# Row factors of two chunks by a VectorE block transpose and DMA instead of matmuls, with the first values tile moved

## The chip, the cores and the metric

One core of one Trainium2 chip. The metric is the device time of one execution in microseconds. The kernel before takes 206.06 us (median of the first three runs, 206.0 to 206.29).

## The reference, cut to what matters

```python
def _B_ref(x, w1, w2, w3, w4):
    h = _gelu(_layernorm(x, axis=-1) @ w1)
    ...                                   # shifts over rows, w2, a second layer norm, w3, w4
x = A_x
xn = _layernorm(x, axis=-1)
s = _A_ref(xn, A_wqkv, A_wo)              # dilated sliding-window attention
g = _silu(_B_ref(xn, B_w1, B_w2, B_w3, B_w4))
return x + s * g
```

x is 2048 rows by 512. The layer norm is applied twice in a row ahead of w1: once for xn and once more inside `_B_ref`. The second one is a factor for each row alone, since the mean of xn is zero. The kernel works in four chunks of 512 rows and holds xn transposed (features over partitions), so a factor for each row is a factor for each *column* there: it has to be turned from one value per partition into one row, repeated over all 128 partitions.

## The kernel before: the parts concerned

```python
def ln_again(c):                     # the factors of chunk c, [128, 4], a column for each tile
    ...
    eng = nc.vector if c == 3 else nc.gpsimd
    ...                              # r2 = rstd*rstd*var + EPS, small operations
    r2b = small.tile([P, TPC], BF16, name="r2b", tag="r2b")
    nc.gpsimd.tensor_tensor(out=r2b, in0=r2, in1=nhalf, op=ALU.pow)      # "the power"
    r2s[c] = r2b

def stage_r(c):                      # turn and spread by four matmuls, then a ScalarE copy
    rp = psb("rrep_ps")
    r2 = r2s.pop(c)
    for j in range(TPC):
        nc.tensor.matmul(rp[:, j * P : (j + 1) * P],
                         lhsT=r2[:, j : j + 1].to_broadcast([P, P]), rhs=ident[:],
                         start=True, stop=True)
    nc.scalar.copy(out=xn2T[c][:, ND - 1, :], in_=rp)

def stage_m(c):                      # "the multiplication": input of w1
    ...                              # rrep = xn2T[c][:, ND - 1, :], the row; cs: columns of chunk c
    nc.vector.tensor_tensor(out=xn2T[c], in0=xnT[p][:, :, cs],
                            in1=rrep.unsqueeze(1).to_broadcast([P, ND, CH]), op=ALU.mult)

# ... program order of the prologue, cut
    turn_dma(2)()                    # xn of chunk 2 to DRAM and back by a DMA transpose
    ln_again(2)
    stage_w1(0, 1)
    mask_full(1)
    mask_fill(0, (0,))               # "the fill copies": two VectorE copies of 128x2048
    for a in range(2):
        qk_pair(1, a)[0]()
    stage_r(1)
    stage_m(1)
    ln_stats(3, 0, 2)
    ...
    stage_w1(1, 0)
    stage_w1(1, 1)
    stage_r(2)
    stage_t(3, 0)                    # transposes of chunk 3 on TensorE
    ln_norm(3, slice(1, 2))
    stage_m(2)
    ln_again(3)
    qk_pair(2, 0)[0]()
    ...
    stage_w1(2, 0, lambda: stage_r(3))
    ...
    va = values(0, 0)                # then the first scores
```

In the timelines the instructions of VectorE and of TensorE start in this order.

The softmax here doesn't subtract the row's maximum and nothing guards it: scores larger than these inputs give would overflow.

## Time and profile before

| | before |
|---|---|
| span in the profile | 204.1 us |
| TensorE busy | 96% |
| VectorE, ScalarE, GpSimd busy | 66%, 64%, 37% |
| first scores start | 46.52 us |

```profile
2.81 0.69 DVE L304 BATCH_NORM_STATS2 l0s<-arena 128x6 f32<-128x512 bf16 x1 [0.90 <-DMA arena<-in_A_x_dram]
46.52 0.42 PE L567 MATMUL s_ps<-arena 32*128 32x128 bf16 x16
```

### The profile page before, as it was taken

The numbers are of one execution on the slowest core, as the hardware profiler recorded it, in microseconds if no ns is written. First come the engines' busy times: TensorE is split into PE (matmuls) and PEld (weight loads), VectorE is DVE, ScalarE is ACT, GpSimd is POOL, SyncE is SP. The second block draws the span as 40 slices with busy tenths as digits, with TensorE's granted clock in tenths as the row PEclk, the third lists the DMA queues.
The fourth block names the chain that finished last, engine by engine and source line by source line (L and its number), as shares of the span: only waits on it lengthen the run. The fifth ranks groups of instructions, "written<-read, shape, count | busy, mean of one in ns | idle before, by whom it ended". The sixth has DMA issues, their size and how long they took to land.

```text
span 204.1 us, 4800 instructions
## 1 busy us (share of the span) xinstructions
PE 195.2 (96%) x1900; PEld 94.9 (47%) x1928; DVE 135.0 (66%) x256; ACT 131.5 (64%) x157; POOL 74.5 (37%) x149
## 2 busy tenths in 40 slices
PE   7899999999999999999999999999999999999990
PEld 2585445444444444444444444444555444444440
DVE  5788897626298988856930101288577968888693
ACT  2366768657988888896556657898788877212130
POOL 5889842100023095964691000003830590700000
PEclk9999999999999999999999999999999999999997
DMA  5992264577900089495798948794220241553312
GB/s 146 356 348 80 87 139 86 85 109 112 275 34 5 14 199 140 75 254 107 181 196 184 295 148 136 109 278 156 36 51 5 56 89 26 116 165 118 117 51 77
DMA packets 33197, 26.74 MB, mean 131 GB/s; under 512 B 14600, under 2 KB 31088, under 8 KB 33176
## 3 DMA queue, kind: packets, MB, share of 16 engines
q1 hardware_dynamic: 30984, 23.22, 44.8%
q0 software_dynamic: 2048, 3.09, 8.9%
q8 instruction: 15, 0.25, 0.5%
q10 hardware_dynamic: 144, 0.13, 0.2%
q14 instruction: 6, 0.05, 0.1%
HBM read 12.40 MB, written 4.98 MB: 85 GB/s over the span
## 4 chain that ended last, share of the span: by engine, by line
PE 71%; DVE 11%; DMA 9%; issue 3%; POOL 3%; ACT 2%; SPq 0%; DVEq 0%; POOLq 0%
PE w_ps L501 19%; PE w_ps L521 10%; PE v_ps L547 8%; PE s_ps L567 7%; PE w_ps L457 6%; PE qk_ps L401 5%; PE w_ps L434 5%; PE o_ps L590 4%; PE qk_ps L419 4%; DMA den_d<-orw 3%; PE wo_ps L683 3%; DMA arena<-rden_d 2%; DVE arena L537 2%; DMA rden_d<-rb 1%; DVE arena L691 1%
## 5 line engine op out<-in xcount | busy, mean ns | idle before, releaser
L572 ACT ACTIVATE arena<-s_ps 128x960 bf16<-128x960 f32 (+1 forms) x68 | 62.7, 975 | 13.7 <-PE s_ps L567 13.7
L521 PE MATMUL w_ps<-arena 128*128 128x512 bf16 (+1 forms) x156 | 38.5, 380 | 0.6 <-issue 0.2
L506 ACT ACTIVATE arena<-w_ps 128x1024 bf16<-128x1024 f32 x20 | 20.5, 1024 | 14.5 <-PE w_ps L501 13.1
L632 POOL DMA_DIRECT2D arena<-orw x48 | 25.0, 528 | 5.8 <-DVE orw L602 5.8
L501 PEld LDWEIGHTS <-arena 128*128 128x128 bf16 (+1 forms) x176 | 17.5, 100 | 20.5 <-issue 0.4
L521 PEld LDWEIGHTS <-arena 128*128 128x128 bf16 (+1 forms) x176 | 16.5, 98 | 19.5
L693 POOL TENSOR_TENSOR arena<-arena 128x512 bf16<-128x512 bf16 x6 | 7.7, 1302 | 44.4 <-DVE arena L691 44.4
L536 ACT ACTIVATE sig<-arena 128x512 bf16<-128x512 bf16 x16 | 10.1, 631 | 21.0 <-DVE arena L527 20.9
L551 DVE CAST v_aug<-v_ps 128x512 bf16<-128x512 f32 x17 | 11.7, 690 | 15.4 <-PE v_ps L547 15.3
L602 DVE CAST orw<-o_ps 128x960 bf16<-128x960 f32 (+1 forms) x17 | 19.7, 1156 | 3.1 <-PE o_ps L590 3.0
L401 PE MATMUL qk_ps<-arena 128*128 128x512 bf16 (+1 forms) x109 | 20.4, 332 | 0.5 <-ACT arena L321 0.3
L501 PE MATMUL w_ps<-arena 128*128 128x512 bf16 (+1 forms) x86 | 19.4, 379 | 0.2
L501 PE MATMUL w_ps<-arena,arena 128*128 128x512 bf16 (+1 forms) x86 | 19.1, 379 | 0.1
L547 PE MATMUL v_ps<-wv_sb,arena 128*128 128x512 bf16 x67 | 17.5, 380 | 0.1
L567 PEld LDWEIGHTS <-arena 32*128 32x128 bf16 x544 | 10.2, 92 | 14.8 <-issue 14.7
L567 PE MATMUL s_ps<-arena 32*128 32x120 bf16 (+1 forms) x544 | 16.1, 213 | 0.1
L527 DVE TENSOR_TENSOR arena<-w_ps,arena 128x512 bf16<-128x512 f32 x16 | 11.0, 686 | 7.9 <-PE w_ps L521 7.9
L273 POOL TENSOR_SCALAR l3r<-l3m 128x1 f32<-128x1 f32 (+1 forms) x10 | 2.4, 238 | 37.6 <-DVE l3m L282 37.6
L457 PE MATMUL w_ps<-arena 128*128 128x512 bf16 x63 | 15.2, 380 | 0.1
L660 DVE TENSOR_TENSOR arena<-arena,orw 128x1440 bf16<-128x1440 bf16 (+1 forms) x2 | 1.6, 783 | 19.8 <-DMA orw<-rden_d 19.8
L434 PE MATMUL w_ps<-arena 128*128 128x512 bf16 x63 | 14.6, 379 | 0.0
L401 PEld LDWEIGHTS <-arena 128*128 128x128 bf16 x112 | 10.6, 98 | 7.9 <-DMA arena<-in_A_wqkv_dram 0.8
(99 smaller groups left out, 273.4 us busy)
## 6 DMA issues: line engine op xcount, KB each, us to landing
x1n_dram<-arena SPq DMA_DIRECT2D x5, 512.0 KB, 3.0
arena<-in_A_x_dram SPq DMA_DIRECT2D x4, 512.0 KB, 6.1
arena<-in_A_x_dram SPq DMA_DIRECT2D x6, 256.0 KB, 6.6
out_dram<-arena SPq DMA_DIRECT2D x6, 256.0 KB, 3.6
arena<-in_B_w_dram SPq DMA_DIRECT2D x1, 1376.0 KB
arena<-in_B_w_dram SPq DMA_DIRECT2D x1, 1280.0 KB
arena<-arena SPq DMA_DIRECT2D x16, 72.0 KB, 2.6
arena<-arena SPq DMA_DIRECT2D x16, 68.0 KB, 4.0
```

What stands on the lines that cost most here:

```text
L401: nc.tensor.matmul(pt[:, b, hh * w : (hh + 1) * w], lhsT=wqk_sb[:, dt, nt * P : (nt + 1) * P], rhs=xnT[p][:, dt, k * CH + hh * w : k * CH ...
L434: nc.tensor.matmul(pt[:, b, :], lhsT=w1_sb[:, dt, g * P : (g + 1) * P], rhs=xn2T[c][:, dt, :], start=(dt == 0), stop=(dt == ND - 1),)
L457: nc.tensor.matmul(pt, lhsT=w2_src(p, g, m0), rhs=w2_sb[:, g, :], start=(g == 0), stop=(g == ND - 1))
L501: nc.tensor.matmul(pt[:fs, ft % 2, :], lhsT=w3_sb[:, dt, ft * P : ft * P + fs], rhs=x1nT[c][:, dt, :], start=(dt == 0), stop=(dt == ND - 1),)
L506: nc.scalar.activation(h3(c, 2 * a, 2), pt, AF.Gelu_apprx_tanh)
L521: nc.tensor.matmul(pt, lhsT=h3(c, ft, 1)[:fs, 0, jj * P : (jj + 1) * P], rhs=w4_sb[:fs, ft, :], start=(ft == 0), stop=(ft == NF - 1),)
L547: nc.tensor.matmul(vp[:nk, :], lhsT=xnT[p][:, dt, k0 : k0 + nk], rhs=wv_sb[:, dt, :], start=(dt == 0), stop=(dt == ND - 1),)
L551: nc.vector.tensor_copy(out=va[:nk, :, 0:DH], in_=vp[:nk, :].rearrange("p (h d) -> p h d", d=DH))
L567: nc.tensor.matmul(st[:nk, b, i * nq : (i + 1) * nq], lhsT=kT[e][r : r + 32, dt, k0 : k0 + nk], rhs=qT[e][r : r + 32, dt, q0 : q0 + nq], s ...
L572: nc.scalar.activation(prv[:nk, 2 * h : 2 * h + 2], st[:nk, :, 0 : 4 * nq], AF.Exp, scale=SCALE)
L602: nc.vector.tensor_copy(out=orw[p, r][:, :, :, q0 - ra : q0 - ra + nq], in_=op[:, :, 0 : 4 * nq].rearrange("p j (s q) -> p j s q", q=nq),)
L632: nc.gpsimd.dma_start(out=oT[p][DH * hh : DH * (hh + 1), :, ra : ra + rw], in_=orw[p, r][32 * cg : 32 * cg + DH, jj],)
```

## The change

It takes the row spread of chunks 1 and 2 off TensorE. The four columns of factors are written into columns 0, 32, 64 and 96 of a zeroed 128x128 tile; one VectorE transpose by 32x32 blocks makes four rows of them; one DMA writes these to DRAM, a second reads them back over all partitions. The first values tile is moved from before the first scores to the place where chunk 2's spread was, and chunk 3's factors ahead of chunk 2's multiplication. The diff, cut:

```diff
+    def row_turn(c):
+        turned = small.tile([P, TPC, 32], BF16, name=f"r2t{c}", tag="r2t", bufs=1)
+        nc.vector.transpose(out=turned..., in_=r2w...)
+        row = dram.tile([TPC, P], BF16, name=f"r2_d{c}")
+        nc.sync.dma_start(out=row.rearrange("t (g i) -> g t i", g=4), in_=turned[0:P:32])
+        r2s[c] = row
+    def row_fill(c):
+        nc.sync.dma_start(out=xn2T[c][:, ND - 1, :], in_=r2s.pop(c)...to_broadcast([P, CH]))
...
     stage_t(1, 1)
+    row_turn(1)
+    row_fill(1)
...
-    turn_dma(2)()
+    turn = turn_dma(2)
     ln_again(2)
     stage_w1(0, 1)
     mask_full(1)
     mask_fill(0, (0,))
+    row_turn(2)
+    turn()
+    row_fill(2)
     for a in range(2):
         qk_pair(1, a)[0]()
-    stage_r(1)
     stage_m(1)
...
-    stage_r(2)
+    va, v_out = values(0, 0, True)
     stage_t(3, 0)
     ln_norm(3, slice(1, 2))
+    v_out()
+    ln_again(3)
     stage_m(2)
-    ln_again(3)
...
-    va = values(0, 0)
```

A start value of a counter also changes, so that the PSUM tiles still alternate.

More of the change, by code (lines that the diff above doesn't have):

```diff
@@ L113 @@
     sg_at = (61, 66, B0 + 33.5)
-    cnt = {"v": 0, "p": 0, "b": 0, "r": 0, "g": 0}
+    cnt = {"v": 0, "p": 0, "b": 1, "r": 0, "g": 0}
     def pst(tag, name):
@@ L331, in ln_norm @@
                 )
+    r2w = small.tile([P, TPC, 32], BF16, name="r2w", tag="r2w", bufs=1)
+    nc.vector.memset(r2w[:], 0.0)
+    def row_turn(c):
+        turned = small.tile([P, TPC, 32], BF16, name=f"r2t{c}", tag="r2t", bufs=1)
+        nc.vector.transpose(
+            out=turned.rearrange("q t i -> q (t i)"), in_=r2w.rearrange("q t i -> q (t i)")
+        )
+        row = dram.tile([TPC, P], BF16, name=f"r2_d{c}")
+        nc.sync.dma_start(
+            out=row.rearrange("t (g i) -> g t i", g=4),
+            in_=turned[0:P:32],
+        )
+        r2s[c] = row
+    def row_fill(c):
+        nc.sync.dma_start(
+            out=xn2T[c][:, ND - 1, :],
+            in_=r2s.pop(c).rearrange("t q -> (t q)").unsqueeze(0).to_broadcast([P, CH]),
+        )
     def ln_again(c):
@@ L340, in ln_again @@
         eng.tensor_scalar(out=r2, in0=r2, scalar1=EPS, scalar2=None, op0=ALU.add)
-        r2b = small.tile([P, TPC], BF16, name="r2b", tag="r2b")
+        if c in (1, 2):
+            r2b = r2w[:, :, 0]
+        else:
+            r2b = small.tile([P, TPC], BF16, name="r2b", tag="r2b")
         with nc.allow_low_precision("bf16 factors"):
@@ L539, with values @@
     orw = {}
-    def values(p, u):
+    def values(p, u, later=False):
         q0, nq, k0, nk = units[u]
@@ L550, in values, with evict @@
             )
-        nc.vector.tensor_copy(
-            out=va[:nk, :, 0:DH], in_=vp[:nk, :].rearrange("p (h d) -> p h d", d=DH)
-        )
+        def evict():
+            nc.vector.tensor_copy(
+                out=va[:nk, :, 0:DH], in_=vp[:nk, :].rearrange("p (h d) -> p h d", d=DH)
+            )
+        if later:
+            return va, evict
+        evict()
         return va
```

## The prediction

> **What bounds the kernel now.** I read the page first: busy shares, the 40 slices, the chain that ended last, and then, for the prologue that the change touches, the timeline of each engine, the list of waits and the one-microsecond windows.
>
> ```profile
> PE 195.2 (96%) x1900; PEld 94.9 (47%) x1928; DVE 135.0 (66%) x256; ACT 131.5 (64%) x157; POOL 74.5 (37%) x149
> PE   7899999999999999999999999999999999999990
> PEclk9999999999999999999999999999999999999997
> ```
>
> TensorE is busy 96% of a 204.1 us span, at full clock, and only the first and last slices fall short. So the time is the sum of TensorE's work from about 10 us to the end, plus what TensorE waits. A change in the prologue counts only by the matmuls it takes from this stream and by the waits it removes or adds.
>
> The prologue's TensorE timeline (start, duration, line, shape, count):
>
> ```profile
> 23.69 0.39 PE L375 MATMUL rrep_ps<-ident,r2b 128*128 128x128 bf16 x4
> 23.92 3.62 PE L401 MATMUL qk_ps<-arena 128*128 128x512 bf16 x16
> 30.82 0.39 PE L375 MATMUL rrep_ps<-ident,r2b 128*128 128x128 bf16 x4
> 31.05 0.61 PE L353 MATMUL tr_ps<-ident,arena 128*128 128x128 bf16 x8
> 35.39 1.03 PE L434 MATMUL w_ps<-arena 128*128 128x512 bf16 x4
> 36.70 0.40 PE L375 MATMUL rrep_ps<-ident,r2b 128*128 128x128 bf16 x4 [0.28 <-POOL r2b L343]
> ```
>
> L375 is the row spread of a chunk's factors by four matmuls (stage_r). Durations overlap, so the cost of a group is the step to the next start: 23.92 - 23.69 = 0.23 us for chunk 1, 31.05 - 30.82 = 0.23 us for chunk 2. The last line, chunk 3, waited for the power of its factors on GpSimd. A matmul of 512 columns takes 0.216 us in this stream (16 in 27.37 - 23.92 = 3.45 us), so four end at 35.39 + 0.86 = 36.25, and the wait really cost 36.70 - 36.25 = 0.45 us (the 0.28 is less because modelled ends overhang). This is the only real wait of TensorE between 11 and 46 us.
>
> VectorE and GpSimd around chunk 1's multiplication (L385, stage_m):
>
> ```profile
> 23.78 1.29 DVE L244 COPY arena<-arena 128x2048 bf16<-128x2048 bf16 x2
> 24.00 1.11 POOL L340 TENSOR_SCALAR r<-r 128x4 f32<-128x4 f32 x1
> 25.19 1.04 POOL L343 TENSOR_TENSOR r2b<-r,nhalf 128x4 bf16<-128x4 f32 x1
> 25.60 1.22 DVE L385 TENSOR_TENSOR arena<-arena 128x2048 bf16<-128x2048 bf16 x1 [0.53 <-ACT arena L379]
> 26.28 1.41 SPq L364 DMA_TRANSPOSE arena<-x1n_dram  x1
> 27.37 0.38 PE L434 MATMUL w_ps<-arena 128*128 128x512 bf16 x1
> ```
>
> Today L385 for chunk 1 waits 0.53 us for ScalarE's copy of the spread row, ends at 26.82, and the w1 matmuls that need it (L434) start at 27.37 with 0.5 us to spare. Chunk 2's factors come out of GpSimd only at 25.19 + 1.04 = 26.23; today nobody needs them before 30.82.
>
> **What the Trainium skill says.** "VectorE: DVE Perf Modes", section "The three transpose paths", gives 311 ns for the VectorE transpose of 128x128 bf16, by 32x32 blocks. No such instruction is in this trace; I use 0.31 us, and about 0.23 for what it adds between neighbours, since neighbours here start 0.08 to 0.1 us before the previous one ends. "SBUF — State Buffer", section "Who interferes with whom", says that a VectorE copy in a two-port mode, or a VectorE instruction with two SBUF inputs, keeps a GpSimd instruction that reads SBUF fully blocked. The trace agrees: L340 takes 0.23 us elsewhere (17.23) and 1.11 beside the fill copy, ending at 25.11, just after the copy (25.07). "PSUM — Partial Sum Buffer", section "Engine vs sequencer instructions", says VectorE's queue is strict FIFO; the timeline shows VectorE starts in program order. "DMA: Bandwidth & Descriptors", section "Anatomy of one DMA — SWDGE (gpsimd) path", gives about 2.0 us fixed per transfer; this trace's transfers of 22.5 KB from the sync queue land in 1.7 us (dn from den_d), so two in series are about 4 us.
>
> **The change, part by part.**
>
> 1. Removed: eight matmuls and their weight loads, 0.23 + 0.23 = 0.46 us of TensorE, all on the bounding stream. Also two ScalarE copies (L379, 0.60 and 0.58 us) off that stream.
>
> 2. Chunk 1's row. Its factors are ready at 17.55 + 1.04 = 18.59. The transpose stands behind the transpose eviction (18.71 + 0.69 = 19.40), so it ends near 19.7. Write and broadcast read, about 2 us each with DMA idle there, land near 24. The row is in time. But the transpose pushes everything behind it on VectorE, and the GpSimd chain fed by it, by 0.23: chunk 2's factors now come at 26.23 + 0.23 = 26.46.
>
> 3. Chunk 2's turn stands on VectorE ahead of stage_m(1). This is the step I think decides. VectorE is done with the fills at 25.07 + 0.23 = 25.30, then waits for chunk 2's factors until about 26.5. Transpose, 0.23 until the next can start: 26.73. stage_m(1), 1.22: ends 27.95, against 26.82 before. TensorE, 0.22 earlier for the removed group, reaches w1 of chunk 1 at 27.15 and waits until about 28.0: a new wait of 0.85 us.
>
> 4. The first values tile (four matmuls, 0.86 us) only moves from 45.56 to before the transposes of chunk 3. Sum zero. It shelters those transposes: their first half needs L328, 30.64 before, about 31.8 after, while TensorE arrives at 28.0 + 3.45 + 0.86 = 32.3.
>
> 5. ln_again(3) moves ahead of stage_m(2). With VectorE some 1.1 us late and the eviction of values added (0.69), the small operations end near 34.5, then stage_m(2) until 35.7 and the fill copies until 36.9. stage_r(3) is due on TensorE at 28.0 + 3.45 + 0.86 + 0.44 + 1.73 + 0.44 + 1.73 + 0.86 = 37.5. The power takes 1.04 us alone, but GpSimd will stand behind stage_m(2), which has two SBUF inputs, and perhaps behind the copies too. Between the two: ready at 36.7, no wait, 0.45 saved; behind both: in the kernel before, it ended 0.86 after the fill copies (36.64 against 35.78), so 37.8 here, a wait of about 0.3, and 0.15 saved. I take 0.3 saved.
>
> 6. The sync queue: the row write waits for the turn (26.8), so the DMA transpose of chunk 2 is issued near 27.4 instead of 26.28. With the 4.8 us median to landing it lands by 32.2; q/k of chunk 2 need it at 32.8. The head mask spreads start near 29.8 instead of 27.81; a spread issue takes 0.6 us, so the second eight, behind the fill at 36.9, are issued by 42 and land by 45, before the first scores at 46.5. Hidden, with 0.6 and 1.5 us to spare.
>
> Sum: -0.46 (matmuls) + 0.85 (new wait) - 0.3 (chunk 3's power) = +0.1 us. 206.06 + 0.1 gives 206.15, rounded.
>
> **Rivals.**
>
> A. All gain, no new wait: -0.46 - 0.45 = -0.9, giving 205.15. For it: the matmuls are really on the path and every other engine is below 70%. Against: strict order on VectorE puts a transpose whose input is late ahead of the multiplication TensorE needs next, and only 0.33 us of slack (27.15 - 26.82) stands against a delay of 1.13.
>
> B. DMA replaces the wait: the delayed DMA transpose lands late, or two row transfers take 3 us each beside it. Estimated 0.5 to 1.5 us more, giving 206.7 to 207.7. For it: 0.6 us is thin, and DMA is busy from 28 to 31. Against: part of that traffic is the spreads, which now come after the transpose.
>
> C. ScalarE at the seam. With values moved away, the table load and first exponential start about 0.8 us later relative to the first scores. Now exponentials of the first scores end at 49.71; then near 50.5, just when the next scores are due (50.5). At most 0.2 us, giving 206.3. TensorE's next work would not be held longer, since ScalarE has a fifth of its time free afterwards.
>
> D. The wait of step 3 is shorter because GpSimd gets its operations in between the fill copies: up to 0.9 us earlier, giving near 205.3. Against: L340 ended only after both copies.
>
> **Range and chances.** The terms are each under 1 us: A and D bound the gain at 0.9, B the loss at 1.5, and repeats spread by 0.3 us (206.0 to 206.29). So 205.3 to 206.9 at 8 in 10. Two per cent is 4.1 us; the part of the chain touched has no such sum, so within 2% is 0.98. A faster result of that size would need a wait that I do not see, a slower one a DMA stall of 4 us.
>
> **What would show it right or wrong.** Right: no L375-type groups for chunks 1 and 2; VectorE idle about 1.2 us near 25.3 ahead of the second transpose, released by GpSimd; TensorE idle about 0.7 to 0.9 us ahead of w1 of chunk 1 near 28.0, released by VectorE; the values matmuls just before chunk 3's transposes; the wait on the power at chunk 3 gone or shorter; first scores within 0.3 us of 46.5. Wrong: no idle of TensorE near 27 to 28 (rival A or D); a wait of q/k on the DMA transpose (B); a gap before the second scores (C); or a transpose much over 0.31 us, which would enter step 3 twice.

## More of the kernel before

The start of the first scores is the best yardstick for a change in the prologue: all its gains and losses lie before it. It is counted from VectorE's first statistics, since the first input lands at another time in each profile.

## The result, and the profile after

206.13 us (median of 6 runs, 205.66 to 206.91); the kernel before in the same rounds 206.13 us. The ratio is 1.0000, 95% interval 0.9977 to 1.0022. Eight matmuls and a wait are gone from an engine that is 96% busy, and the time is the same.

The start of VectorE's first statistics, then the TensorE timeline of the changed kernel (start, duration, line, shape, count; L458 is w1, L425 q/k, L571 values, L377 transposes, L399 the remaining row spread, L596 scores):

```profile
3.03 0.69 DVE L304 BATCH_NORM_STATS2 l0s<-arena 128x6 f32<-128x512 bf16 x1 [1.13 <-DMA arena<-in_A_x_dram]
20.45 7.07 PE L425 MATMUL qk_ps<-arena 128*128 128x512 bf16 x31
28.24 3.61 PE L458 MATMUL w_ps<-arena 128*128 128x512 bf16 x16 [0.72 <-DVE arena L409]
31.69 1.03 PE L571 MATMUL v_ps<-wv_sb,arena 128*128 128x512 bf16 x4
32.55 0.61 PE L377 MATMUL tr_ps<-ident,arena 128*128 128x128 bf16 x8
33.00 1.89 PE L425 MATMUL qk_ps<-arena 128*128 128x512 bf16 x7
36.90 1.03 PE L458 MATMUL w_ps<-arena 128*128 128x512 bf16 x4
37.76 0.39 PE L399 MATMUL rrep_ps<-ident,r2b 128*128 128x128 bf16 x4
46.72 0.42 PE L596 MATMUL s_ps<-arena 32*128 32x128 bf16 x16
```

The q/k group runs through where the row spread of chunk 1 stood. It is 32 matmuls (the trace lost one record), and at 0.216 us each ends at 20.45 + 6.91 = 27.36. w1 starts at 28.24: a new wait of 0.88 us, released by VectorE's multiplication. (The 0.72 in brackets is less because the modelled end of the last matmul overhangs; this wait is counted by steps between starts.) At 37.76 the row spread of chunk 3 follows without a wait. The first scores start at 46.72 against 46.52, but the first input also landed later in this profile: VectorE's first statistics start at 3.03 against 2.81. Counted from there it is 43.69 against 43.71, the same within 0.02 us.

The VectorE and GpSimd timelines around the new wait, and the sync queue:

```profile
24.18 1.29 DVE L244 COPY arena<-arena 128x2048 bf16<-128x2048 bf16 x2
26.68 0.31 DVE L338 STREAM_TRANSPOSE r2t<-r2w 128x128 bf16<-128x128 bf16 x1 [1.21 <-POOL r2w L367]
26.91 1.18 DVE L409 TENSOR_TENSOR arena<-arena 128x2048 bf16<-128x2048 bf16 x1
24.40 1.10 POOL L361 TENSOR_SCALAR r<-r 128x4 f32<-128x4 f32 x1
25.59 1.05 POOL L367 TENSOR_TENSOR r2w<-r,nhalf 128x4 bf16<-128x4 f32 x1
27.65 2.08 SPq L388 DMA_TRANSPOSE arena<-x1n_dram  x1
34.69 2.30 POOL L367 TENSOR_TENSOR r2b<-r,nhalf 128x4 bf16<-128x4 f32 x1 [2.18 <-DVE r L361]
```

After the fill copies VectorE stands idle for 1.21 us. Its next instruction is the turn of chunk 2, whose factors GpSimd delivers only at 26.64. The multiplication that TensorE wants stands behind the turn, though its own data are there: in e1 it runs right after the copies. (The last line, chunk 3's power, is for the part on the prediction.) GpSimd is late because L361, elsewhere 0.23 us, took 1.10 beside the fill copies.

### The profile page after: what moved, and what is told of

It is laid out like the page before. It is cut to its first block, busy times and chain, and to the rows that moved or that the text cites. A ratio compares the mean times of both kernels' runs of the same rounds, so it can differ in the third digit from the quotient of the medians.

```text
span 203.9 us, 4790 instructions
## 1 busy us (share of the span) xinstructions
PE 193.4 (95%) x1892; PEld 94.0 (46%) x1920; DVE 135.2 (66%) x259; ACT 130.5 (64%) x155; POOL 75.1 (37%) x149
## 4 chain that ended last, share of the span: by engine, by line
PE 74%; DVE 9%; DMA 9%; POOL 4%; issue 2%; ACT 0%; SPq 0%; DVEq 0%
PE w_ps L525 19%; PE w_ps L545 10%; PE v_ps L571 8%; PE w_ps L481 7%; PE s_ps L596 7%; PE w_ps L458 6%; PE qk_ps L425 5%; PE o_ps L619 4%; PE qk_ps L443 4%; DMA den_d<-orw 3%; PE wo_ps L712 3%; DMA arena<-rden_d 2%; DMA rden_d<-rb 2%; DVE arena L561 2%; DVE arena L720 1%
## 5 line engine op out<-in xcount | busy, mean ns | idle before, releaser
L425 PE MATMUL qk_ps<-arena 128*128 128x512 bf16 (+1 forms) x109 | 20.2, 332 | 0.7 <-ACT arena L321 0.5
L571 PE MATMUL v_ps<-wv_sb,arena 128*128 128x512 bf16 x66 | 17.4, 380 | 0.1
L596 PEld LDWEIGHTS <-arena 32*128 32x128 bf16 x544 | 10.2, 92 | 14.5 <-issue 14.4
L551 DVE TENSOR_TENSOR arena<-w_ps,arena 128x512 bf16<-128x512 f32 x16 | 11.0, 686 | 7.9 <-PE w_ps L545 7.9
L596 PE MATMUL s_ps<-arena 32*128 32x120 bf16 (+1 forms) x544 | 15.9, 213 | 0.0
L458 PE MATMUL w_ps<-arena 128*128 128x512 bf16 x63 | 14.6, 379 | 0.7 <-DVE arena L409 0.7
L485 DVE TENSOR_TENSOR arena<-w_ps,arena 128x512 bf16<-128x512 f32 x16 | 10.4, 684 | 7.2 <-PE w_ps L481 7.2
```

Of the source, the lines that this page charges most:

```text
L425: nc.tensor.matmul(pt[:, b, hh * w : (hh + 1) * w], lhsT=wqk_sb[:, dt, nt * P : (nt + 1) * P], rhs=xnT[p][:, dt, k * CH + hh * w : k * CH ...
L458: nc.tensor.matmul(pt[:, b, :], lhsT=w1_sb[:, dt, g * P : (g + 1) * P], rhs=xn2T[c][:, dt, :], start=(dt == 0), stop=(dt == ND - 1),)
L571: nc.tensor.matmul(vp[:nk, :], lhsT=xnT[p][:, dt, k0 : k0 + nk], rhs=wv_sb[:, dt, :], start=(dt == 0), stop=(dt == ND - 1),)
L596: nc.tensor.matmul(st[:nk, b, i * nq : (i + 1) * nq], lhsT=kT[e][r : r + 32, dt, k0 : k0 + nk], rhs=qT[e][r : r + 32, dt, q0 : q0 + nq], s ...
```

## The experiments

All gave correct results. Runs of the kernel before: 206.04 us for e1 to e4, 206.13 for e5 to e8 (one of its 11 runs at 207.25), 206.08 for e9 and e10. The three calls ran on three chips, so across calls the ratios are compared, not the medians.

| run | median us (range) | ratio to before (95%) |
|---|---|---|
| changed kernel | 206.13 (205.66 to 206.91) | 1.0000 (0.9977 to 1.0022) |
| e1 | 206.06 (205.93 to 206.37) | 1.0003 (0.9990 to 1.0015) |
| e2 | 205.21 (204.85 to 205.86) | 0.9951 (0.9938 to 0.9965) |
| e3 | 205.17 (205.08 to 205.27) | 0.9955 (0.9943 to 0.9968) |
| e4 | 205.54 (205.50 to 206.07) | 0.9979 (0.9967 to 0.9992) |
| e5 | 206.37 (205.79 to 207.79) | 1.0024 (0.9995 to 1.0053) |
| e6 | 206.40 (205.54 to 207.37) | 1.0005 (0.9978 to 1.0033) |
| e7 | 205.57 (205.24 to 206.00) | 0.9966 (0.9947 to 0.9985) |
| e8 | 204.89 (204.80 to 205.07) | 0.9932 (0.9915 to 0.9948) |
| e9 (changed kernel again) | 205.97 (205.76 to 206.09) | 0.9986 (0.9974 to 0.9998) |
| e10 (e6 again) | 205.66 (205.44 to 205.85) | 0.9975 (0.9962 to 0.9987) |

### e1: the multiplication of chunk 1 ahead of the turn of chunk 2

```diff
     mask_fill(0, (0,))
+    stage_m(1)
     row_turn(2)
     turn()
     row_fill(2)
     for a in range(2):
         qk_pair(1, a)[0]()
-    stage_m(1)
```

> The changed kernel with chunk 1's multiplication ahead of chunk 2's turn on VectorE, nothing else. Theory (the 0.7 to 0.9 us that TensorE waits ahead of w1 of chunk 1 comes from the order on VectorE, and is what eats the gain): no wait of TensorE at that place, multiplication starting near 25.5 instead of 26.9, time about 0.85 us below the changed kernel, 205.3 us, ratio to the kernel before about 0.996. Rival 1 (the DMA transpose of chunk 2, still issued behind the row write, becomes the bound since TensorE now comes 0.85 us earlier to the q/k of chunk 2): TensorE waits 0.2 to 0.6 us there and the time is 205.5 to 205.9. Rival 2 (the equal time comes from something later in the kernel): 206.1, ratio 1.000.

Measured: 206.06 us, no gain. By the time alone rival 2 would have it; the profile decides. The TensorE, GpSimd and sync queue timelines of e1:

```profile
27.41 3.62 PE L458 MATMUL w_ps<-arena 128*128 128x512 bf16 x16
33.29 1.89 PE L425 MATMUL qk_ps<-arena 128*128 128x512 bf16 x8 [0.95 <-DMA arena<-x1n_dram]
25.65 1.92 POOL L367 TENSOR_TENSOR r2w<-r,nhalf 128x4 bf16<-128x4 f32 x1
28.58 2.16 SPq L388 DMA_TRANSPOSE arena<-x1n_dram  x1
```

The wait ahead of w1 is gone, as the theory said. In its place q/k of chunk 2 wait 0.95 us for the DMA transpose: rival 1, and larger than its bounds. Counted by steps, as the 0.88 us were, it is 1.11 us (the transposes start at 31.73, the next start follows 0.45 later where nothing waits, as in e8, and q/k start at 33.29), and the first scores come at 47.00 - 3.07 = 43.93 from the first statistics, 0.24 later than in the changed kernel. It has two causes. TensorE comes 0.88 us earlier. And the DMA transpose starts 0.93 us later than in the changed kernel (28.58 against 27.65): it stands on the sync queue behind the row write, the row write waits for the turn, the turn for the power, and the power now took 1.92 instead of 1.05 us. The multiplication had started at 25.44, just ahead of the power, and ended at 26.66.

### e2: as e1, with the DMA transpose issued ahead of the row write

```diff
     stage_m(1)
-    row_turn(2)
     turn()
+    row_turn(2)
     row_fill(2)
```

> As the run before, and the DMA transpose of chunk 2 issued ahead of the row write on the sync queue. Theory: as that run, 205.3 us; the DMA transpose starts near 26.4 instead of 27.65. If rival 1 of that run holds, this one is 0.2 to 0.6 us faster than it; if not, the two are equal within 0.1 us. Rival: the row of chunk 2 now comes late behind the transpose, and the multiplication of chunk 2 and w1 of chunk 2 wait, making it slower than the run before.

Measured: 205.21 us, 0.85 below e1, more than the 0.2 to 0.6 expected. So rival 1 of e1 held, and both waits are real: each alone hides the gain. But the rival of e2 shows too, in small. Its VectorE, TensorE and sync queue timelines:

```profile
35.07 1.23 DVE L409 TENSOR_TENSOR arena<-arena 128x2048 bf16<-128x2048 bf16 x1 [0.81 <-DMA arena<-r_d]
36.36 1.04 PE L458 MATMUL w_ps<-arena 128*128 128x512 bf16 x4 [0.25 <-DVE arena L409]
26.93 2.19 SPq L388 DMA_TRANSPOSE arena<-x1n_dram  x1
29.22 0.56 SPq L342 DMA_DIRECT2D r_d<-r2t  x1
```

The row write is ready at 27.8 but is issued at 29.22, since issuing the DMA transpose holds the sync queue for 2.19 us. Chunk 2's multiplication waits 0.81 us for the row, and TensorE 0.25 by the profile, 0.41 by steps: the first scores come at 46.18 - 2.94 = 43.24, against 42.82 in e8, which has no wait.

### e3: chunk 2's row by matmuls again

```diff
     mask_fill(0, (0,))
-    row_turn(2)
     turn()
-    row_fill(2)
...
     stage_w1(1, 0)
+    stage_r(2)
     stage_w1(1, 1)
```

(The factors of chunk 2 go back into a tile of their own, and the counter for PSUM tiles starts at 0.)

> The changed kernel with only chunk 1 by turn and DMA; chunk 2's row by four matmuls again, placed between the two halves of w1 of chunk 1. Theory: the 0.88 us wait goes, 0.23 us of matmuls come back: 0.65 below the changed kernel, 205.5 us, ratio to before 0.997. Rival (the wait was not caused by chunk 2's turn): 206.1 or above.

Measured: 205.17 us, 0.0045 below before in the ratio, somewhat more than expected. TensorE has no wait between 11 us and the end. Half of the change, without chunk 2's turn and with both moves, is faster than the whole. In this profile one small GpSimd operation of chunk 2's factors took 3.30 us instead of 0.36 (23.41 to 26.71, across VectorE's fill copies and multiplication); it cost nothing, since the matmuls ask for these factors only at 29.14.

### e4: the moves alone

```diff
     stage_w1(1, 0)
+    stage_r(2)
     stage_w1(1, 1)
-    stage_r(2)
+    va, v_out = values(0, 0, True)
     stage_t(3, 0)
     ln_norm(3, slice(1, 2))
-    stage_m(2)
+    v_out()
     ln_again(3)
+    stage_m(2)
```

(And no values tile before the scores. To keep the PSUM tiles apart, chunk 2's row spread moved ahead of the second half of w1.)

> The kernel before with the moves alone (values tile and chunk 3's factors earlier), both rows by matmuls as before. Theory: the 0.45 us wait on chunk 3's power goes, nothing else changes: 205.7 us, ratio 0.998. Rival (that wait was hidden or is replaced by a later one): 206.1, ratio 1.000.

Measured: 205.54 us, 0.50 below before: the 0.45 us wait on chunk 3's power is worth its full length when it is removed alone. The first scores agree: 46.17 - 2.91 = 43.26, against 43.71 before.

### e5: the turns alone, without the moves

```diff
-    va, v_out = values(0, 0, True)
     stage_t(3, 0)
     ln_norm(3, slice(1, 2))
-    v_out()
-    ln_again(3)
     stage_m(2)
+    ln_again(3)
...
+    va = values(0, 0)
```

> The changed kernel without the two moves: values tile back before the first scores, chunk 3's factors back behind the multiplication of chunk 2. Theory: the wait of 0.88 us ahead of w1 of chunk 1 stays, and the wait on chunk 3's power (0.4 to 0.5 us) comes back, perhaps with 0.1 to 0.3 us ahead of the transposes of chunk 3, which the values tile no longer shelters: 0.5 to 0.8 us above the changed kernel, 206.6 to 206.9 us, ratio 1.002 to 1.004. Rival (the moves gave nothing beside the turns): 206.1.

Measured: 206.37 us, spread over 2 us, interval 0.9995 to 1.0053: the time does not decide. The profile does, and against the theory. Its TensorE and GpSimd timelines:

```profile
28.07 3.61 PE L458 MATMUL w_ps<-arena 128*128 128x512 bf16 x16 [0.72 <-DVE arena L409]
36.81 0.39 PE L399 MATMUL rrep_ps<-ident,r2b 128*128 128x128 bf16 x4
35.10 1.38 POOL L367 TENSOR_TENSOR r2b<-r,nhalf 128x4 bf16<-128x4 f32 x1 [2.77 <-DVE r L361]
```

The wait ahead of w1 stays, but the wait on chunk 3's power did not come back: it ends at 36.48, and TensorE arrives at 36.81. Counted from the first statistics, TensorE comes 0.51 us later than in the kernel before (33.95 against 33.44), which alone is more than the 0.45 us it waited there, and the power ends 0.21 us earlier (33.62 against 33.83). The 0.51 are about the new wait of 0.88 less the 0.46 of removed matmuls, and a gap of 0.08 ahead of the transposes of chunk 3, which the values tile no longer shelters. So in the changed kernel the moves gave only about that much: first scores count 46.62 - 2.86 = 43.76 from the first statistics, against 43.69 there.

### e6 and e10: who holds the power in e1

```diff
     mask_fill(0, (0,))
+    nc.vector.bn_stats(out=spare[:], in_=xn[1][:, 0, :])
     stage_m(1)
     row_turn(2)
```

(Cut: the tile `spare`, and the later `stage_m(1)`, which goes as in e1.)

> The first experiment (multiplication of chunk 1 ahead of the turn) with one spare statistics instruction of 0.66 us put ahead of the multiplication, its result unused. Theory (in the first experiment GpSimd's power of chunk 2 took 1.92 instead of 1.05 us because the multiplication, with two SBUF inputs, started 0.2 us before it and held it): now the power starts first and takes 1.05 us, the turn of chunk 2 starts near 27.1 instead of 27.6, the DMA transpose 0.5 us earlier, and the wait of q/k on it falls from 0.95 to about 0.45 us: 205.6 us although one instruction more runs. Rival (the power was held by something else): the power stays at 1.9 us, wait and time as in the first experiment, 206.1 us, or worse.

Measured: 206.40 us, from 205.54 to 207.37, and a profile that answers another question: a small operation three steps ahead of the power took 2.17 us, so that the power started at 26.19, again behind the multiplication (25.98), and took 1.91. By itself inconclusive, so it ran again unaltered:

> The experiment with the spare statistics instruction once more, unaltered: its profile had an operation of GpSimd held 2.17 us before the power, which spoilt the comparison. Theory (that is a matter of the run): if the profile falls on a run without it, the power starts near 25.6, ahead of the multiplication, takes 1.05 us, and q/k wait about 0.45 us on the DMA transpose; runs again spread by over 1 us with the fastest near 205.5. Rival (the spare instruction causes the 2.17 us every time): the same profile again and all runs at 206.4.

GpSimd in e6, then TensorE, GpSimd, VectorE and the sync queue in e10:

```profile
23.34 2.17 POOL L360 TENSOR_TENSOR r<-l1r 128x2 f32<-128x2 f32 x1
26.19 1.91 POOL L368 TENSOR_TENSOR r2w<-r,nhalf 128x4 bf16<-128x4 f32 x1
```

```profile
32.64 1.89 PE L426 MATMUL qk_ps<-arena 128*128 128x512 bf16 x7 [0.36 <-DMA arena<-x1n_dram]
25.59 1.05 POOL L368 TENSOR_TENSOR r2w<-r,nhalf 128x4 bf16<-128x4 f32 x1
25.99 1.20 DVE L410 TENSOR_TENSOR arena<-arena 128x2048 bf16<-128x2048 bf16 x1
28.08 2.14 SPq L389 DMA_TRANSPOSE arena<-x1n_dram  x1
```

Measured in e10: 205.66 us, all runs 205.44 to 205.85. With the power 0.4 us ahead of the multiplication it takes 1.05 us, the DMA transpose starts 0.50 us earlier than in e1, the wait falls from 0.95 to 0.36 by the profile, and the kernel is faster (ratio 0.9975 against 1.0003) although one instruction was added. The theory holds: started behind the multiplication (e1, e2, e6, e7) the power takes 1.9 us, started ahead of it (before, changed, e10) 1.05. The Trainium skill, "SBUF — State Buffer", section "Who interferes with whom", says that the order of issue decides who blocks; these six profiles and that of the kernel before agree.

The expectation that all runs of e10 would spread by over 1 us failed: they spread by 0.41. The rival that the spare instruction causes the 2.17 us every time is out: it did not in e10, and in e3 the same operation took 3.30 us without it.

### e7: as e2, chunk 2's row transfers on ScalarE's queue

```diff
+    def row_turn(c, q=nc.sync): ...      # q.dma_start; row_fill likewise
     stage_m(1)
     turn()
...
     qk_pair(1, 2)[0]()
+    row_turn(2, nc.scalar)
...
     stage_w1(1, 0)
+    row_fill(2, nc.scalar)
```

(Cut: the first issues of the mask spreads on the sync queue move ahead of the q/k pair before the turn.)

> The second experiment (multiplication first, DMA transpose issued early) with chunk 2's two row transfers issued by ScalarE's queue instead of behind the DMA transpose on the sync queue. Theory (the 0.25 us of TensorE and 0.81 us of VectorE left there come from the row write standing behind a 2.2 us issue of the DMA transpose): the row is in by 33, the multiplication of chunk 2 waits for nothing, 0.25 us less: 204.95 us, ratio 0.994. Rival (ScalarE is held while it waits for the turn and the row, and its copies come late): new waits on ScalarE, 205.3 or more.

Measured: 205.57 us, a miss in time and what the rival had written, on the chip whose runs spread most. In its profile the mechanism is partly right: VectorE waits 0.28 us for the row instead of 0.81, TensorE not at all, and first scores start at 45.83, no later than in e8 counted from the first input. The rival shows as well: ScalarE does no work for 2.0 us while its queue waits for the turn and issues the row write, though the first scores do not come later for it. The time was lost later: against e8 0.28 us at a group of scores at 153.7 us and some 0.4 us in the last 15 us. Why is open.

### e8: fill copies behind the multiplication

```diff
-    mask_fill(0, (0,))
+    ln_stats(3, 0, 2)
     row_turn(2)
     turn()
     row_fill(2)
     for a in range(2):
         qk_pair(1, a)[0]()
     stage_m(1)
-    ln_stats(3, 0, 2)
+    mask_fill(0, (0,))
```

> The changed kernel with its order of turn and multiplication kept, but the mask fill copies of 1.29 us moved behind the multiplication and two statistics pairs of chunk 3 put in their place. Theory (chunk 2's factors are late because the fill copies hold GpSimd's small operation for 1.1 us): that operation takes about 0.25 us, the power ends near 25.8, the turn starts near 25.9, the multiplication ends by 27.3, TensorE does not wait ahead of w1 of chunk 1, the DMA transpose starts near 26.7 and q/k do not wait: 205.0 to 205.25 us, ratio 0.995. Rival (the fill copies are not what holds GpSimd): the turn stays near 26.7 and the time at 206.1.

GpSimd, VectorE, sync queue and TensorE of e8:

```profile
24.32 0.23 POOL L361 TENSOR_SCALAR r<-r 128x4 f32<-128x4 f32 x1
24.64 1.05 POOL L367 TENSOR_TENSOR r2w<-r,nhalf 128x4 bf16<-128x4 f32 x1
25.72 0.31 DVE L338 STREAM_TRANSPOSE r2t<-r2w 128x128 bf16<-128x128 bf16 x1
25.95 1.19 DVE L409 TENSOR_TENSOR arena<-arena 128x2048 bf16<-128x2048 bf16 x1
26.70 2.13 SPq L388 DMA_TRANSPOSE arena<-x1n_dram  x1
27.29 3.61 PE L458 MATMUL w_ps<-arena 128*128 128x512 bf16 x16
32.05 1.89 PE L425 MATMUL qk_ps<-arena 128*128 128x512 bf16 x8
45.76 0.42 PE L596 MATMUL s_ps<-arena 32*128 32x128 bf16 x16
```

Measured: 204.89 us, all six runs within 0.27 us, ratio 0.9932: 1.24 us under before and the best of all. Every step came as written, and the time a little below the 205.0 to 205.25 expected. The small operation takes 0.23 instead of 1.10 us, the turn needs no wait, and the multiplication ends at 27.14, before TensorE needs it. It is the changed kernel with only the order of two groups on VectorE swapped, and it brings what the change was made for. First scores: 45.76 - 2.94 (start of the first statistics) = 42.82, which is 0.87 below the changed kernel: the new wait and nothing else. The hold on GpSimd did not vanish but moved to two operations of chunk 3, beside the multiplication and the copies (1.60 us instead of 0.71, 0.92 instead of 0.40), for which nothing near waits. By the ratios the kernels are 1.4 us apart, 1.1 us with the runs of e9. In the profiles a further 0.2 us lies in the last 15 us, on VectorE: the last matmuls differ by 0.95 us (0.09 of it later input), the last VectorE instruction by 1.15. In the changed kernel the chain that ended last runs through the DMA transfers of the last softmax normalisation, in e8 it does not; what of this comes again in each run was not tested.

### e9: the changed kernel again

> The changed kernel itself once more, unaltered. Its six runs spread over 1.25 us, those of the kernel before over 0.35. Theory (the wait ahead of w1 of chunk 1 is longer in some runs, since GpSimd's small operations ahead of chunk 2's power lose their gap between VectorE's instructions in some runs and not in others): again runs from 205.7 to about 207, mean ratio to before 1.000 to 1.003; if this profile falls on a longer run, an operation of GpSimd ahead of the power takes over 2 us and TensorE waits over 1.2 us. Rival (spread of the chip on that day): runs within 0.4 us, near 206.1.

Measured: 205.97 us, 205.76 to 206.09; the profile shows the same 1.21 us of VectorE and the same start of w1 (28.21). The wide spread of the first six runs did not return, so that theory has no support from this run. The profiles of e6 and e3 show that GpSimd's chain can come late in a single run: counted from the first statistics the power of chunk 2 starts at 23.18 and 24.32 there, against 22.56 in the changed kernel. Whether that made the wide ranges of the first runs and of e5 stays open.

## Why the prediction was right, step by step

- **Removed matmuls, 0.46 us: right.** w1 could have started at 27.36 - 0.22 (later input) = 27.14, against 27.37 before, 0.23 for chunk 1. For chunk 2, e3 has the four matmuls that e8 has not: first scores at 46.12 - 3.08 = 43.04 against 42.82, 0.22 us, each counted from its first statistics.
- **New wait of 0.85 us: right, 0.88 measured.** VectorE idle 1.21 us where 1.2 was written, released by GpSimd, the turn 0.31 us long and 0.23 until its neighbour. e8 removes it by removing its cause, and gains all of it.
- **Chunk 3's power, 0.3 saved: the size was off, and the reason too.** The whole 0.45 us went, since there is no wait at 37.76. The power did stand behind both the multiplication and the fill copies (2.30 us, ending at 36.99, against 36.95 for the copies), as the worse case had it, but ended 0.04 after them and not 0.86. Why it ended so soon after them is not shown. And e5 shows that beside the new wait the power's wait vanishes even without the move, since TensorE then comes 0.51 us later. The prediction treated the two terms as independent; they overlap. In e4, which has no new wait, the move is worth its 0.45 us.
- **Row transfers, "about 4 us" for two in series: too short beside the other transfers, and hidden.** The 1.7 us were among the shortest of such transfers in that trace, where they took 1.6 to 3.9. From the issue of the write to the start of the multiplication that waits for the row it took 29.22 to 35.07 = 5.85 us in e2 and 27.89 to 34.62 = 6.73 us in e7, so rival B's 3 us each is nearer. In the changed kernel the multiplication of chunk 2 comes only at 34.52, 7.50 us after the write was issued, and did not wait.
- **Sum.** -0.46 + 0.88 - 0.45 = -0.03 us, where +0.1 was predicted; the profile has -0.02 at the first scores.
- **The rivals. A (all gain)** is what e8 reaches: 42.82 against 43.71 at the first scores, 0.89 us where 0.9 was estimated, and 1.24 in the medians. **Rival B (DMA in its place)** did not occur in the changed kernel, but stood 0.6 us behind, as written: from issue to first use the DMA transpose takes 4.7 us where it is awaited (33.29 - 28.58 in e1), so in the changed kernel it landed near 32.4 for a use at 33.0. e1 uncovered it. **Rival C** cost nothing that lasted: the second scores take 0.51 instead of 0.42 us, but by 53.45 TensorE is again 0.19 us behind the kernel before (53.26), as it was 0.20 behind at the first scores. That ScalarE is the cause was not tested. **Rival D** (GpSimd between the copies) did not occur.
- **The range** held: 205.3 to 206.9, with one of six runs at 206.91.

## What to carry to other kernels

When work moves from the bounding engine to an in-order one, look at what stands behind it in that queue: an instruction whose input is late holds up later ones that are ready, and here gave back all of 0.9 us. Removing the first wait can show a second of equal size close behind it (e1), so test the pair and not each alone. A small GpSimd operation in a chain that matters belongs beside VectorE instructions that leave it alone, such as statistics (0.23 us in e8), and not beside copies (1.10) or two-input multiplications (the power: 1.9 instead of 1.05).

## What the Trainium skill lacked or had wrong

- "SBUF — State Buffer", section "Who interferes with whom": right in the rule, but a blocked GpSimd operation need not get in at the end of the one instruction that blocks it. It stayed blocked over two copies in a row (1.10 instead of 0.23 us) and twice over a longer run of VectorE instructions (2.17 us in e6 and 3.30 in e3, instead of 0.36).
- "DMA: Bandwidth & Descriptors", section "DMA Transpose (X-bar)": it has no figure for how long the issue of a DMA transpose of this size holds its queue. Issuing one of 512 KB held the sync queue 1.41 us for chunk 2 in the kernel before and 2.0 to 2.2 us for chunk 2 in the kernels with row transfers, and delayed the 1 KB write behind it by 1.4 us (e2). The row transfers need not be the reason: the later ones in the kernel before took 1.92 to 3.21 us.
- "TensorE: Matmul & The Clock Gate", section "Back-to-back issue gap": it gives about 131 ns for a matmul of 512 columns in a sustained stream with weight loads. Here such a stream runs at 216 ns each (16 in 3.45 us), and the transposes and row spreads of 128 columns at about 57 ns (four in 0.23 us), which is what the page calls the isolated gap.
- "VectorE: DVE Perf Modes", section "The three transpose paths": 311 ns, measured 301 to 311. What it lacks is what it costs between neighbours: 0.23 us.
